# Fused band-and-summary attention with a GELU layer pair: the second layer of the last two chunks as seven products of quarters, and a new order of the early steps

## The chip, the core and the metric

The kernel runs on one core of a Trainium2 chip. The metric is the time of one launch in microseconds (us), measured on the device, as the median of several runs; lower is better. The core's engines work side by side from queues of their own: PE (TensorE, matmuls; its weight loads are listed apart as PEld), DVE (VectorE), ACT (ScalarE), POOL (GpSimd) and SP (SyncE, which here issues all transfers). Matmuls write to PSUM (tiles named `ps...`); the other tiles lie in SBUF.

## The reference

`q`, `k` and `v` have the shape 4 x 8 x 768 x 64 (batch, heads, positions, head width). Every query sees the keys less than 16 positions away and, besides, one summary of each block of 32 keys. The result, 3072 tokens of 512, goes through two layers with a GELU between.

```python
k_sum = k.reshape(B, H, nb, block, D).max(axis=3)
v_sum = v.reshape(B, H, nb, block, D).mean(axis=3)
scores_l = scale * np.matmul(q, k.transpose(0, 1, 3, 2))
scores_s = scale * np.einsum('bhsd,bhnd->bhsn', q, k_sum) + np.log(block)
scores_all = np.concatenate([np.where(mask_l, scores_l, -1e9), scores_s], axis=-1)
a = np.exp(scores_all - np.max(scores_all, axis=-1, keepdims=True))
a = a / (np.sum(a, axis=-1, keepdims=True) + 1e-09)
x = np.matmul(a, np.concatenate([v, v_sum], axis=2))       # to 3072 x 512
h = x @ w_in                                               # 512 x 2048
g = 0.5 * h * (1.0 + erf(h * inv_sqrt2))
out = g @ w_out                                            # 2048 x 512
```

## The kernel before

**Numbers.** Most operands of a matmul are f32 values split into two f16 values, a high part and the rest (`..._hi` on ACT, `..._lo` on DVE), and a product is three matmuls: high x high, high x low, low x high. The weights arrive as 64-bit floats and are put together on DVE in three steps of bit work each (`wi_bits`, `wo_bits`, lines 348 to 357).

**Tiles.** The attention is done in 24 units of 256 queries and 4 heads (`Unit`). The two units of 256 tokens make a chunk, so there are 12 chunks; six units make one of the four batches of the input. The attention of units 0 to 5 (`N_F32`) runs in f32 (`f_scores`, `f_sums`, `f_values`), that of the others in f16 pairs (`scores`, `sums`, `values`). Between them stand the maximum over partitions on POOL (`maximum`, L726), the shift on DVE (`shift`, L731), the exponent on ACT (`exponent`, L734) and the division (`norm_take`, `norm_rec`, `norm_spread` and `norm_mult` on DVE, L799 to L816). `x_hi` and `x_lo` (L820, L823) split the result.

**First layer.** Chunks 0 to 3 take `phase1` (L843 to L845): 24 matmuls of 256 columns for each of 8 blocks of `w_in`. Chunks 4 to 11 go in pairs (`STRASSEN`): the 512 tokens by 512 inputs of a pair are four quarters, and each part q of four (512 of the 2048 outputs) takes seven products `sp b q n` (L914, 12 matmuls of 256 columns each) in place of eight. Sums of inputs are `xsum`, `xs_hi`, `xs_lo`; sums of weights `wt_add`, `wt_hi`, `wt_lo`. The products of one part gather in three PSUM banks x, y and z; `snap` (ACT, L925) copies y in between, `comb` (DVE, L932) adds. Then `s_gelu` (L939), `sg_hi` (ACT, L942) and `sg_lo` (DVE, L946) put the result into `gg`.

**Second layer.** `phase2 c i` (L960 to L962) takes part i // 2 of chunk c for 128 of its 256 tokens: 12 matmuls of 512 columns. Eight such steps make a chunk; `store` (ACT, L967) copies the PSUM bank and `put` sends it.

**The order.** The string `ORDER` lists all steps by name. They are issued in that order, so it is the order of every engine's queue and of SP's transfers; waits between engines follow from the tiles. Buffers with a count (`f4k` has four) can be written again when the last reader of one is done.

**Front.** In the first 120 us the weights are made, the first units are computed and `phase1` begins. `fetch_w_in`, `fetch_k`, `fetch_v`, `fetch_vt` and `load_q`, `load_k`, `load_v` are transfers on SP's queue; `prep_k` and `prep_v` reduce blocks on DVE; `wi_diff` and `wi_dlo` make the low part of a weight block on PE and ACT in place of `wi_lo` on DVE.

## Time and profile before

| | us |
|---|---|
| median of three runs | 607.15 (604.36 to 607.5) |
| the profiled execution | 603.98 |
| its span, first to last instruction | 602.2 |
| PE busy, of the span | 578.3 (96%) |
| DVE busy | 420.2 (70%) |
| ACT busy | 351.1 (58%) |
| POOL busy | 90.2 (15%) |

The profile has one execution. Busy PE counts each matmul to its modelled end, and matmuls overlap: one of 512 columns is listed with 379 ns, while the next starts much sooner, so the time of a step on PE is read from start to start. The chain of waits follows back from the last instruction what released each one. `L960` is line 960 of the kernel. Groups are written as `line engine operation out<-in`, then the count, the busy time, the mean of one, and the idle time before them with what ended it.

### The profile page before, as it was taken

How to read it: one execution, taken by the hardware profiler on the slowest of the kernel's cores; microseconds unless marked ns; L12 is line 12 of the kernel's file. 1: busy time of each engine (PE TensorE's matmuls, PEld its weight loads, DVE VectorE, ACT ScalarE, POOL GpSimd, SP SyncE). 2: the span in 40 equal slices, each digit the busy share in tenths (PEclk: the TensorE clock that was granted, in tenths of full speed). 3: DMA queues.
4: the chain of work that ended last, by engine and by line, in shares of the span. 5: the costliest groups of instructions: out<-in, count | busy, mean ns of one | idle time of the engine just before them, and what ended most of it. 6: DMA issues, size and time to landing. Idle time of an engine off the chain costs nothing.

```text
span 602.2 us, 12775 instructions
## 1 busy us (share of the span) xinstructions
PE 578.3 (96%) x5532; PEld 378.2 (63%) x5532; DVE 420.2 (70%) x567; ACT 351.1 (58%) x508; POOL 90.2 (15%) x41
## 2 busy tenths in 40 slices
PE   3988989999999999999999999999999999999997
...
DVE  4999999798878889788978646956367655134110
...
GB/s 315 370 356 267 270 124 253 130 178 112 127 130 111 112 77 120 64 145 75 126 25 112 40 60 59 118 63 51 45 85 2 19 19 19 19 1 19 17 19 35
DMA packets 28216, 64.47 MB, mean 107 GB/s; under 512 B 2688, under 2 KB 6528, under 8 KB 28160
## 3 DMA queue, kind: packets, MB, share of 16 engines
...
q14 instruction: 13, 0.11, 0.1%
...
## 4 chain that ended last, share of the span: by engine, by line
PE 87%; DVE 6%; issue 3%; DMA 2%; POOL 1%; ACT 1%; SPq 0%; POOLq 0%; ACTq 0%; DVEq 0%
PE psy L914 14%; PE pso L960 14%; PE pso L962 14%; PE pso L961 14%; PE psz L914 7%; PE psh L843 4%; PE psh L844 4%; PE psh L845 4%; PE psx L914 4%; PE psv L779 3%; PE pss L703 2%; PE psv L792 2%; DMA v<-in_vw_dram 1%; DVE wt L353 1%; DMA x32s<-in_w_out_dram 1%
## 5 line engine op out<-in xcount | busy, mean ns | idle before, releaser
L960 PE MATMUL pso<-w_out_h,gg 128*128 128x512 f16 x384 | 145.7, 379 | 0.7 <-ACT ot L967 0.7
L962 PE MATMUL pso<-w_out_h,gg 128*128 128x512 f16 x384 | 145.5, 379 | 0.0
L961 PE MATMUL pso<-w_out_l,gg 128*128 128x512 f16 x384 | 145.5, 379 | 0.0
L726 POOL PARTITION_ALL_REDUCE m<-s x24 | 83.4, 3473 | 354.3 <-DVE s L717 126.0
L914 PEld LDWEIGHTS <-wt 128*128 128x128 f16 x768 | 74.4, 98 | 14.0 <-issue 1.7
L843 PE MATMUL psh<-xos,ww 128*128 128x256 f16 x256 | 70.3, 275 | 0.0
L844 PE MATMUL psh<-xos,ww 128*128 128x256 f16 x256 | 70.2, 274 | 0.0
L914 PE MATMUL psy<-xos,wt 128*128 128x256 f16 x576 | 69.9, 273 | 0.2 <-ACT ww L925 0.2
L845 PE MATMUL psh<-xos,ww 128*128 128x256 f16 x256 | 70.1, 274 | 0.0
L946 DVE SCALAR_TENSOR_TENSOR gg<-g,gg 128x512 f16<-128x512 f32 x64 | 45.6, 727 | 29.8 <-ACT gg L942 29.6
L962 PEld LDWEIGHTS <-gg 128*128 128x128 f16 x384 | 37.6, 98 | 45.3
L914 PEld LDWEIGHTS <-ww 128*128 128x128 f16 x576 | 55.2, 98 | 12.7 <-issue 2.5
L960 PEld LDWEIGHTS <-gg 128*128 128x128 f16 x384 | 37.5, 98 | 40.3 <-issue 0.8
L961 PEld LDWEIGHTS <-gg 128*128 128x128 f16 x384 | 37.6, 98 | 39.7 <-issue 1.0
L925 ACT ACTIVATE ww<-psy 128x512 f32<-128x512 f32 x48 | 28.0, 590 | 46.2 <-PE psy L914 44.6
L967 ACT ACTIVATE ot<-pso 128x512 f32<-128x512 f32 x24 | 14.3, 596 | 58.0 <-PE pso L962 58.0
L932 DVE TENSOR_TENSOR g<-psz,ww 128x512 f32<-128x512 f32 x32 | 22.0, 686 | 31.0 <-PE psz L914 26.1
L939 ACT ACTIVATE g<-g 128x512 f32<-128x512 f32 x48 | 29.8, 624 | 21.3 <-DVE g L932 21.1
L942 ACT ACTIVATE gg<-g 128x512 f16<-128x512 f32 x64 | 38.8, 622 | 3.5 <-PE pso L961 2.9
L731 DVE TENSOR_TENSOR s<-s,m 128x1024 f32<-128x1024 f32 x24 | 29.2, 1217 | 9.5 <-POOL m L726 9.5
L734 ACT ACT_TABLE_LOAD x20 | 25.7, 1283 | 10.6 <-DVE s L731 10.3
L799 DVE STREAM_TRANSPOSE dent<-psv 128x512 f32<-128x512 f32 x24 | 17.1, 712 | 17.0 <-PE psv L792 11.1
...
## 6 DMA issues: line engine op xcount, KB each, us to landing
...
gg<-in_w_in_dram SPq DMA_DIRECT2D x6, 1024.0 KB
...
vb<-in_vb_dram SPq DMA_DIRECT2D x12, 384.0 KB
xos<-in_w_out_dram SPq DMA_DIRECT2D x4, 1024.0 KB
```

What stands on the lines that cost most here:

```text
L726: nc.gpsimd.partition_all_reduce(out_ap=self.m32, in_ap=self.s32, channels=P, reduce_op=bass_isa.ReduceOp.max)
L731: nc.vector.tensor_tensor(out=self.s32, in0=self.s32, in1=self.m32, op=ALU.subtract)
L843: nc.tensor.matmul(ph[:, e, :], wh, xh, start=(k == 0), stop=False)
L844: nc.tensor.matmul(ph[:, e, :], wh, xl, start=False, stop=False)
L845: nc.tensor.matmul(ph[:, e, :], wl, xh, start=False, stop=(k == NCC - 1))
L914: nc.tensor.matmul(ps[:, e, :], ws, xx, start=(first and e == 0 and k == 0 and m == 0), stop=(k == 1 and m == 2), skip_group_check=True,)
L939: nc.scalar.activation(dst, src, AF.Gelu, scale=1.0 / (SC_X * SC_WI))
L942: nc.scalar.activation(g_part(o // 2, q, 0, slice(o % 2, 4, 2)), g32t[b, q, o], AF.Copy, scale=SC_G)
L946: nc.vector.scalar_tensor_tensor(out=g_part(o // 2, q, 1, fs), in0=g32t.pop((b, q, o)), scalar=SC_G, in1=g_part(o // 2, q, 0, fs), op0=ALU ...
L960: nc.tensor.matmul(p, gh, w_out_h[:, f, :], start=(f == 0), stop=False)
L961: nc.tensor.matmul(p, gh, w_out_l[:, f, :], start=False, stop=False)
L962: nc.tensor.matmul(p, gl, w_out_h[:, f, :], start=False, stop=(f == NFC - 1))
```

## The change

The second layer of chunks 10 and 11 (the last pair) is done by seven products of quarters too. For each part q the quarters of A are chunk 10 or 11 by even or odd blocks of 128 of the four in a part; those of B are the same blocks of `w_out` by left or right 256 columns. `so n q j` is product n for 128 tokens: 6 matmuls of 256 columns. All parts gather in four PSUM regions: x and w (the bank pair of the scores), y (that of `phase2`) and z (that of the attention's values). y is copied three times (`o_snap`), `o_sum` adds it to x, z and w, `o_out` is the last copy of y, and `o_put` sends a quarter's half.

The results of the GELU stay in f32 (`h32`) until their sums are made (`h_sum`), and then seven operands a part are split (`h_hi`, `h_lo`) instead of four. They go to rooms of `gg` that chunks 8 and 9 have left and to rooms of `wt`. The weight sums are added up from the high and low parts of `w_out` (`t_sum`, eight steps a part), split (`t_hi`, `t_lo`), and put into buffers that the attention has left: x32s, v32, vh and vl, q32, k32, qh and ql; `dent`, `ph` and `pl` hold them in between. `wo_diff` and `wo_dlo` are defined and not called.

Removed: 16 `phase2`, 4 `store`, 4 `put`, 12 `comb`, 16 each of `s_gelu`, `sg_hi` and `sg_lo`. Added: 56 `so`, 12 `h_comb`, 16 `h_gelu`, 16 `h_sum`, 28 `h_hi`, 28 `h_lo`, 32 `t_sum`, 16 `t_hi`, 16 `t_lo`, 3 `o_snap`, 4 `o_sum`, 2 `o_out`, 8 `o_put`. No other step is removed or added.

The order is new in two places. From the start to just behind `phase1 2 0` (`wo_bits 6 0`) the same steps stand in another order; from there to `xsum 3 1`, which opens the products of chunks 6 and 7, nothing is changed; and from there to the end the order is new.

```diff
-fetch_k 0 0, prep_k 0 0, k_pack 2, fetch_w_in 5 5, load_m16, f_mask 2, wi_bits 5 0, wi_bits 5 1, wi_bits 5 2, wi_hi 5,
-load_eye, load_q 2, f_scores 2, fetch_w_in 3 3, wi_bits 3 0, fetch_v 1 2, prep_k_end 0 0, wi_bits 3 1, prep_v 1 2,
-fetch_w_in 0 0, evac 2, maximum 2, load_q 0, wi_bits 3 2, fetch_k 0 1, wi_bits 0 0, f_mask 0, k_pack 0, wi_bits 0 1,
-wi_hi 3, shift 2, load_neg, wi_bits 0 2, fetch_v 1 0, f_scores 0, prep_v 1 0, fetch_w_in 7 3, evac 0, wi_hi 0, wi_diff
-3 1, wi_diff 0 1, maximum 0, wi_dlo 0 1, wi_diff 3 0, wi_dlo 3 0, prep_k 0 1, wi_bits 7 0, f_mask 1, load_q 1, wi_bits
-7 1, wi_diff 0 0, wi_bits 7 2, k_pack 1, f_scores 1, shift 0, exponent 0, fetch_w_in 2 2, load_ind, wi_bits 2 0,
-wi_bits 2 1, wi_hi 7, evac 1, maximum 1, f_sums 0, wi_dlo 0 0, fetch_vt 1, wi_bits 2 2, wi_hi 2, fetch_vt 0, wi_lo 7,
-sum_vt 0, sum_vt 1, norm_take 0, norm_rec 0, norm_spread 0, wi_lo 5, fetch_vt 2, fetch_w_in 4 4, shift 1, wi_bits 4 0,
-sum_vt 2, load_v 0, mean_vt, s_load_vs 0, k_pack 3, wi_diff 2 1, f_mask 3, f_values 0, wi_diff 2 0, prep_k_end 0 1,
-fetch_w_in 6 2, exponent 1, wi_bits 4 1, wi_bits 4 2, load_v 1, norm_mult 0, f_sums 1, s_load_vs 1, wi_bits 6 0,
-wi_bits 6 1, norm_take 1, norm_rec 1, wi_dlo 2 0, x_hi 0, x_lo 0, norm_spread 1, f_values 1, norm_mult 1, load_q 3,
-f_scores 3, fetch_w_in 1 1, wi_bits 1 0, wi_bits 1 1, load_v 2, exponent 2, x_hi 1, f_sums 2, fetch_k 1 3, norm_take
-2, prep_k 1 3, x_lo 1, evac 3, load_k 4, load_q 4, fetch_w_out 0 4, load_vs 2, f_mask 4, wi_dlo 3 1, f_values 2,
-wi_bits 6 2, maximum 3, fetch_k 1 1, wi_dlo 2 1, load_mask, k_pack 4, phase1 0 3, wi_hi 4, shift 3, norm_rec 2,
-exponent 3, phase1 0 5, wi_hi 6, wi_bits 1 2, wo_bits 0 0, wo_bits 0 1, gelu 0 3, fetch_w_out 1 5, gelu 0 5, f_scores
...
+fetch_k 0 0, prep_k 0 0, prep_k_end 0 0, fetch_w_in 5 5, load_m16, load_q 2, k_pack 2, f_mask 2, f_scores 2, wi_bits 5
+0, wi_bits 5 1, wi_bits 5 2, wt_add 5 0, wt_add 5 1, fetch_vt 0, wi_hi 5, load_eye, load_ind, fetch_w_in 0 0, wi_lo 5,
+k_sums 0 0, sum_vt 0, wt_add 5 2, evac 2, maximum 2, f_mask 0, load_neg, wi_bits 0 0, wi_bits 0 1, k_pack 0, wt_hi 5,
+wt_lo 5, load_q 0, f_scores 0, wi_bits 0 2, fetch_vt 1, fetch_k 0 1, prep_k 0 1, sum_vt 1, prep_k_end 0 1, shift 2,
+evac 0, maximum 0, wi_hi 0, shift 0, exponent 0, k_pack 1, exponent 2, wi_diff 0 0, fetch_vt 2, wi_diff 0 1,
+fetch_w_in 3 3, f_mask 1, load_q 1, fetch_w_in 2 2, sum_vt 2, mean_vt, load_v 0, f_sums 0, wi_bits 3 0, fetch_w_in 4
+4, wi_bits 3 1, f_scores 1, load_q 3, wi_bits 3 2, norm_take 0, wi_hi 3, s_load_vs 0, wi_diff 3 0, wi_bits 2 0,
+wi_bits 2 1, wi_bits 2 2, evac 1, wi_dlo 3 0, load_v 1, norm_rec 0, wi_hi 2, norm_spread 0, f_values 0, norm_mult 0,
+maximum 1, fetch_w_in 7 3, wi_diff 2 1, f_mask 3, wi_dlo 0 1, wi_diff 3 1, k_pack 3, x_hi 0, wi_bits 4 0, wi_bits 4 1,
+wi_dlo 0 0, x_lo 0, shift 1, exponent 1, s_load_vs 1, f_scores 3, wi_bits 4 2, f_sums 1, wi_hi 4, fetch_w_in 1 1,
+wi_bits 7 0, load_v 2, wi_bits 7 1, evac 3, f_values 1, wi_diff 2 0, wi_dlo 2 0, norm_take 1, maximum 3, norm_rec 1,
+norm_spread 1, norm_mult 1, x_hi 1, wi_bits 7 2, fetch_k 1 1, load_k 4, f_mask 4, fetch_w_out 0 4, x_lo 1, wi_dlo 2 1,
+f_sums 2, norm_take 2, prep_k 1 1, fetch_k 1 2, phase1 0 5, wi_hi 7, phase1 0 2, gelu 0 2, load_vs 2, f_values 2,
+shift 3, wi_lo 7, norm_rec 2, load_q 4, wi_lo 4, exponent 3, phase1 0 0, norm_spread 2, k_pack 4, wo_bits 0 0, wi_bits
+1 0, norm_mult 2, wo_bits 0 1, wi_bits 1 1, wo_bits 0 2, gelu 0 0, fetch_w_in 6 2, g_hi 0 0, gelu 0 5, f_scores 4,
...
+3, phase2 8 4, phase2 8 6, store 8 0, put 8 0, norm_rec 22, norm_spread 22, t_sum 0 3, snap 5 0 1, norm_mult 22, sg_hi
+4 3 2, sg_lo 4 3 2, sp 5 1 1, snap 5 1 1, xsum 5 1, xsum 5 3, phase2 9 1, phase2 9 3, xs_hi 5 1, t_sum 0 1, xs_hi 5 3,
+xs_lo 5 1, t_sum 0 0, xsum 5 2, xs_lo 5 3, phase2 9 5, xsum 5 4, phase2 9 7, xs_hi 5 4, h_comb 0 0, t_sum 0 2, t_sum 0
+4, t_hi 0 3, t_lo 0 3, xs_hi 5 2, xs_lo 5 2, t_sum 0 5, sp 5 0 6, t_hi 0 1, sp 5 0 5, t_hi 0 2, t_lo 0 2, snap 5 0 2,
...
+h_hi 3 22, h_sum 2 4, so 1 2 1, h_hi 2 4, h_lo 3 11, h_hi 2 2, h_lo 2 2, so 1 3 0, so 1 3 1, sp 5 3 3, h_lo 2 1,
+h_gelu 3 2, so 3 1 0, so 2 2 1, o_snap 1, so 6 0 0, so 3 1 1, t_sum 3 5, t_hi 3 2, t_lo 3 2, h_comb 3 1, h_gelu 3 1,
+so 6 0 1, so 6 1 0, so 6 1 1, so 6 2 0, h_lo 3 22, so 5 1 1, so 5 2 0, so 5 2 1, h_hi 3 12, h_lo 3 12, h_lo 2 4, so 3
+2 0, h_sum 3 1, h_sum 3 3, h_sum 3 2, h_hi 3 2, h_lo 3 2, t_hi 3 3, t_hi 3 1, so 6 2 1, t_lo 3 3, so 6 3 0, so 6 3 1,
+h_hi 3 3, o_snap 2, so 2 3 0, h_lo 3 3, so 2 3 1, so 7 0 0, h_sum 3 4, h_hi 3 4, h_lo 3 4, put 8 1, h_hi 3 1, t_lo 3
+1, h_lo 2 3, so 7 0 1, so 7 1 0, so 7 1 1, so 7 2 0, so 7 2 1, so 7 3 0, so 3 2 1, h_lo 3 1, so 3 3 0, so 7 3 1, so 5
+3 0, so 5 3 1, o_snap 3, so 4 0 0, t_sum 3 6, t_sum 3 7, t_hi 3 4, o_sum 0, o_put 0 1, so 4 1 0, so 4 2 0, o_sum 3,
+o_put 3 1, o_put 3 0, t_lo 3 4, o_sum 4, so 4 3 0, so 3 3 1, o_put 0 0, o_sum 1, o_put 1 0, o_put 1 1, o_out 0, so 4 0
+1, so 4 1 1, o_put 2 0, so 4 2 1, so 4 3 1, o_out 1, o_put 2 1
...
+    b12, t2w, t32f = {}, {}, {}
+    A_ROOM = {11: (0, 0), 12: (0, 1), 22: (1, 1), 1: (1, 0)}
+    def a_part(q, m, z):
+        if m in A_ROOM:
+            c, h = A_ROOM[m]
+            return gg[:, c, q, z, h : FQ : 2, :]
+        room = wt[:, 2 * q : 2 * q + 2].rearrange("p i n -> p (i n)").bitcast(F16)
+        i = (2, 3, 4).index(m) * 4 * CH + z * 2 * CH
+        return room[:, i : i + 2 * CH].rearrange("p (e j) -> p e j", e=2)
+    def h32(q, o):
+        if (L2, q, o) not in g32t:
+            t = wk.tile([P, WP], F32, tag="f4k", bufs=N_F4K, name=f"h32_{q}_{o}")
+            for n in range(2):
+                g32t[L2, q, o // 2 * 2 + n] = t[:, n * 512 : (n + 1) * 512].rearrange("p (e j) -> p e j", e=2)
+        return g32t[L2, q, o]
+    def h_comb(q, o):
+        n, y = {0: (1, "x"), 1: (2, "z"), 3: (3, "z")}[o]
+        nc.vector.tensor_tensor(
+            out=split8(h32(q, o)), in0=split8(acc[L2, q, y]), in1=snaps[L2, q, n], op=ALU.add
+        )
+    def h_gelu(q, o):
+        nc.scalar.activation(
+            h32(q, o), acc[L2, q, "y"] if o == 2 else h32(q, o), AF.Gelu, scale=1.0 / (SC_X * SC_WI)
+        )
+    def h_src(q, m):
+        return h32(q, {11: 0, 12: 1, 22: 3, 1: 3, 2: 0, 3: 2, 4: 1}[m])
+    def h_sum(q, n):
+        a11, a12, a21, a22 = (h32(q, o) for o in range(4))
+        out, in0, in1, op = (
+            (a22, a21, a22, ALU.add),
+            (a11, a22, a11, ALU.subtract),
+            (a21, a11, a21, ALU.subtract),
+            (a12, a12, a11, ALU.subtract),
+        )[n - 1]
+        nc.vector.tensor_tensor(out=flat2(out), in0=flat2(in0), in1=flat2(in1), op=op)
+    def h_hi(q, m):
+        nc.scalar.activation(a_part(q, m, 0), h_src(q, m), AF.Copy, scale=SC_G)
+    def h_lo(q, m):
+        nc.vector.scalar_tensor_tensor(
+            out=a_part(q, m, 1), in0=h_src(q, m), scalar=SC_G, in1=a_part(q, m, 0), op0=ALU.mult, op1=ALU.subtract
+        )
+    def b_part(q, h, n, z):
+        return (w_out_h, w_out_l)[z][:, q * FQ + h : (q + 1) * FQ : 2, n * CH : (n + 1) * CH]
+    def t_room(q, n, z):
+        if (n, q, z) not in t2w:
+            if n == 1:
+                x = flat2(x32s[:, (4, 0, 1, 2)[q]]).bitcast(F16)
+                t2w[n, q, 0], t2w[n, q, 1] = x[:, :512], x[:, 512:]
+            elif n == 2:
+                v = ld.tile([P, UH * CT, D], F32, tag="v32", bufs=N_V32, name=f"t2_{q}")
+                v = v.rearrange("p n d -> p (n d)").bitcast(F16)
+                for i in range(4):
+                    t2w[n, q // 2 * 2 + i // 2, i % 2] = v[:, i * 512 : (i + 1) * 512]
+            elif n == 3:
+                a = wk.tile([P, UCOLS], F16, tag="vh" if q % 2 else "vl", bufs=N_VH, name=f"t3_{q}")
+                t2w[n, q, 0], t2w[n, q, 1] = a[:, :512], a[:, 512:]
+            elif q > 1:
+                t2w[n, q, z] = wk.tile([P, QCOLS], F16, tag=("qh", "ql")[z], bufs=N_QH, name=f"t4_{q}_{z}")
+            else:
+                if q == 0:
+                    a = ld.tile([P, QCOLS], F32, tag="q32", bufs=N_Q32, name="t4_0")
+                else:
+                    a = ld.tile([P, KC * TQ], F32, tag="k32", bufs=N_K32, name="t4_1")
+                a = a.bitcast(F16)
+                t2w[n, q, 0], t2w[n, q, 1] = a[:, :512], a[:, 512:1024]
+        return t2w[n, q, z]
+    def t_sum(q, i):
+        def tmp(k):
+            tag = ("pl", "dent", "ph")[k]
+            if tag == "dent":
+                return wk.tile([P, NR * CH], F32, tag="dent", bufs=1, name=f"tw_{q}_{i}")
+            return wk.tile([P, UCOLS], F16, tag=tag, bufs=N_PH, name=f"tw_{q}_{i}").bitcast(F32)
+        def whole(k, h, n):
+            b12[q, k] = tmp(k)
+            nc.vector.tensor_tensor(
+                out=b12[q, k].rearrange("p (e j) -> p e j", e=2), in0=b_part(q, h, n, 0), in1=b_part(q, h, n, 1), op=ALU.add
+            )
+        def diff(k, i0, i1, op, n):
+            nc.vector.tensor_tensor(out=b12[q, k], in0=b12[q, i0], in1=b12[q, i1], op=op)
+            t32f[n, q] = b12[q, k]
+        if i == 0:
+            whole(0, 0, 1)
+        elif i == 1:
+            whole(1, 1, 1)
+        elif i == 2:
+            diff(1, 1, 0, ALU.subtract, 3)
+        elif i == 3:
+            whole(2, 0, 0)
+        elif i == 4:
+            diff(0, 0, 2, ALU.subtract, 1)
+        elif i == 5:
+            diff(2, 1, 2, ALU.add, 2)
+        elif i == 6:
+            whole(1, 1, 0)
+        else:
+            diff(1, 1, 2, ALU.subtract, 4)
+    def t_hi(q, n):
+        nc.scalar.activation(t_room(q, n, 0), t32f[n, q], AF.Copy)
+    def t_lo(q, n):
+        nc.vector.tensor_tensor(out=t_room(q, n, 1), in0=t32f[n, q], in1=t_room(q, n, 0), op=ALU.subtract)
+    def so(n, q, j):
+        m, w, y = {
+            1: (11, (0, 0), "y"),
+            2: (12, (1, 0), "x"),
+            3: (4, (1, 1), "w"),
+            4: (22, 4, "y"),
+            5: (1, 1, "z"),
+            6: (2, 2, "y"),
+            7: (3, 3, "y"),
+        }[n]
+        first = (L2, y) not in acc
+        if first:
+            if y == "y":
+                t = ps_o.tile([P, DM], F32, tag="pso", name="pso_y")
+            elif y == "z":
+                t = ps_v.tile([P, 2, NR * CH], F32, tag="psv", name="psv_z")[:, 0]
+            else:
+                if "s" not in acc:
+                    acc["s"] = ps_s.tile([P, UCOLS], F32, tag="pss", name="pss_x")
+                t = acc["s"][:, :512] if y == "x" else acc["s"][:, 512:]
+            acc[L2, y] = t.rearrange("p (e j) -> p e j", e=2)
+        ps = acc[L2, y]
+        js = slice(j * P, (j + 1) * P)
+        for e in range(2):
+            gh, gl = (a_part(q, m, z)[:, e, js] for z in range(2))
+            if isinstance(w, int):
+                wh, wl = (t_room(q, w, z).rearrange("p (e n) -> p e n", e=2)[:, e] for z in range(2))
+            else:
+                wh, wl = (b_part(q, *w, z)[:, e] for z in range(2))
+            for k, (g, ww_) in enumerate(((gh, wh), (gh, wl), (gl, wh))):
+                nc.tensor.matmul(
+                    ps[:, j, :], g, ww_, start=(first and e == 0 and k == 0), stop=(e == 1 and k == 2),
+                    skip_group_check=True,
+                )
+    OSC = 1.0 / (SC_G * SC_WO)
+    osn = {}
+    def o_snap(n):
+        osn[n] = g32_tile(("os", n))
+        nc.scalar.activation(flat2(osn[n]), flat2(acc[L2, "y"]), AF.Copy, scale=OSC)
+    def o_sum(o):
+        y, s = {0: ("x", 1), 4: ("z", 2), 3: ("z", 3), 1: ("w", 4)}[o]
+        osn["o", o] = osn[s]
+        if o == 4:
+            osn[4] = osn[2]
+        nc.vector.scalar_tensor_tensor(
+            out=flat2(osn[s]), in0=flat2(acc[L2, y]), scalar=OSC, in1=flat2(osn[s]), op0=ALU.mult, op1=ALU.add
+        )
+    def o_out(j):
+        if j == 0:
+            osn["o", 2] = g32_tile(("os", 5))
+        nc.scalar.activation(osn["o", 2][:, j], acc[L2, "y"][:, j], AF.Copy, scale=OSC)
+    def o_put(o, j):
+        r0 = (2 * L2 + o // 2) * CH + j * P
+        queue[0].dma_start(out=out[r0 : r0 + P, o % 2 * CH : (o % 2 + 1) * CH], in_=osn["o", o][:, j])
```

`xsum` and `xsrc` name the buffers `x32s` directly; they compute the same.

More of the change, by code (lines that the diff above doesn't have):

```diff
@@ L111 @@
+values 6, s_k_hi 8, k_lo 8, gelu 2 5, fetch_k 2 0, load_q 9, s_q_hi 9, phase2 0 6, store 0 0, norm_take 6, add_mask 7,
+norm_rec 6, norm_spread 6, q_lo 9, maximum 7, phase1 2 3, prep_k 2 0, shift 7, load_vs 7, v_hi 7, scores 8, load_k 9,
+v_lo 7, fetch_v 2 1, load_q 11, fetch_k 2 2, exponent 7, phase2 0 1, phase2 0 3, s_p_hi 7, norm_mult 6, put 0 0,
 add_mask 8, prep_k 2 2, s_k_hi 9, phase2 0 5, phase2 0 7, k_lo 9, g_hi 2 4, p_lo 7, values 7, g_lo 2 4, sums 7,
@@ new lines @@
+add_mask 17, values 16, prep_k_end 3 0, k_sums 3 0, sums 16, q_lo 18, xs_hi 3 3, maximum 17, xs_lo 3 3, sp 3 1 6, sp 3
+0 2, comb 3 0 0, phase2 4 1, phase2 4 3, norm_take 16, norm_rec 16, norm_spread 16, s_gelu 3 0 0, sg_hi 3 0 0, xsum 3
+4, load_k 19, shift 17, s_k_hi 19, k_lo 19, exponent 17, load_q 19, prep_v 3 1, xs_hi 3 4, xs_lo 3 4, load_v 18,
+s_q_hi 19, q_lo 19, sp 3 0 7, snap 3 1 2, phase2 4 5, put 5 0, phase2 4 7, sg_lo 3 0 0, scores 18, prep_v 3 3, load_vs
+18, sp 3 1 7, add_mask 18, store 4 1, put 4 1, phase2 5 1, snap 3 0 3, sp 3 0 4, v_hi 18, s_gelu 3 0 2, sg_hi 3 0 2,
```

174 lines of the change are left out of this document (87 added, 87 removed).

## The prediction

> **What bounds the kernel now.** I read the page's share by engine and by line of the chain that ended last, then its 40 slices, then the busy time by stretch over five cuts that I chose, then the chain itself piece by piece around its gaps.
>
> ```profile
> PE 87%; DVE 6%; issue 3%; DMA 2%; POOL 1%; ACT 1%; SPq 0%; POOLq 0%; ACTq 0%; DVEq 0%
> PE   3988989999999999999999999999999999999997
> DVE  4999999798878889788978646956367655134110
> ```
> ```profile
> 0.00:53.10 53.10, 39.36 (x287) 21.85 (x287) 44.62 (x49) 24.86 (x33) 17.79 (x18) 1.00 0.90 318
> 53.10:118.30 65.20, 61.03 (x631) 48.66 (x628) 59.95 (x82) 47.43 (x70) 15.41 (x7) 0.97 0.64 221
> 118.30:233.80 115.50, 115.50 (x1264) 74.57 (x1262) 102.32 (x138) 78.95 (x106) 19.64 (x6) 1.00 0.37 116
> 233.80:480.10 246.30, 244.65 (x2562) 163.52 (x2560) 176.61 (x246) 157.87 (x230) 37.36 (x11) 1.00 0.24 71
> 480.10:602.20 122.10, 117.76 (x801) 69.59 (x799) 36.66 (x56) 41.95 (x71) 0.00 (x0) 1.00 0.05 18
> ```
>
> The columns of the second fence are the stretch, its length, busy PE, weight loads, DVE, ACT and POOL, the granted clock, DMA share and GB/s. The cuts are the first product of the first layer (53.1), the last product ahead of the place where both orders have done the same steps (118.3), the first seven-product step (233.8) and the start of the tail (480.1). From 118.3 on PE is busy almost without a break: there a microsecond of PE work is a microsecond of time. Before 53.1 it is DVE: 44.62 us busy of the 48.1 since its first data came at 5.0 (first row, from the view of waits), and the chain runs down DVE:
>
> ```profile
> DVE ks_f L471 <- DMA w_out_l<-in_kp_dram: 5.0, 1, 5.0
> ```
> ```profile
> 49.24 0.61 DVE wt L348
> 49.88 1.23 DVE wt L353
> 51.10 0.62 DVE dent L799
> 51.73 0.85 DVE ks L471
> ```
>
> The DMA share of 0.90 makes transfers the second bound of that stretch. So the change has two places to act: PE work saved anywhere after 53.1, and DVE work taken out of the front.
>
> **The change: the seven products.** Sixteen `phase2` steps of chunks 10 and 11 go, 12 matmuls of 512 columns each, 192 in all. Fifty-six `so` steps of 6 matmuls of 256 columns come, 336 in all.
>
> ```profile
> 575.67 1.31 PE psx L914 x12
> ```
> ```profile
> 588.02 0.38 PE L960 MATMUL pso<-w_out_h,gg 128*128 128x512 f16 x1 [0.69 <-ACT ot L967]
> ...
> 592.55 0.38 PE L960 MATMUL pso<-w_out_h,gg 128*128 128x512 f16 x1
> ```
>
> The second fence holds the first and last of 22 starts in a row, so 4.53/21 = 0.2157 us for 512 columns. The first has twelve matmuls of 256 columns, each with its own 128x128 weights, in 1.31: 0.109 each. That is the form of `so`. 192 x 0.2157 = 41.4 goes, 336 x 0.109 = 36.7 comes: **-4.7 us**. The cover of the new matmuls is the weight load under them:
>
> ```profile
> L914 PEld LDWEIGHTS <-wt 128*128 128x128 f16 x768 | 74.4, 98 | 14.0 <-issue 1.7
> ```
>
> 98 ns beneath 109 leaves 11. Should a tenth of the load show (10 ns x 336), 3.4 of the 4.7 would be gone.
>
> What feeds the products stands on DVE and ACT of the tail. Rows of that stretch, by groups:
>
> ```profile
> L946 DVE SCALAR_TENSOR_TENSOR gg<-g,gg 128x512 f16<-128x512 f32 x21 | 14.0, 689 | 22.3 <-ACT gg L942 22.3
> L942 ACT ACTIVATE gg<-g 128x512 f16<-128x512 f32 x21 | 12.5, 621 | 0.2
> L875 DVE TENSOR_TENSOR x32s<-x32s 128x512 f32<-128x512 f32 x4 | 2.8, 690 | 0.1
> ```
>
> All new DVE steps work on 512 elements a partition. `h_sum` 16, `t_sum` 32, `t_lo` 16, twelve more `h_lo` than there were `sg_lo`, and 4 `o_sum`: 80 instructions x 0.69 = 55.2. `h_comb` replaces `comb` one for one. A `t_sum` that adds two f16 blocks into f32 is not in the trace. Below, it might take half of a row, 0.35, which would save 16 x 0.35 = 5.6 of DVE; above, the 0.85 that `prep_k` took in the chain, for 768 elements, would add 32 x 0.16 = 5.1. I take 0.69, the like f32 row; neither end reaches PE, as follows. DVE has 36.7 busy in 122.1; it gets 91.9 in 122.1 - 4.7 = 117.4 and keeps **25.5 us free**. ACT gets 12 `h_hi` and 16 `t_hi` at 0.62, and five reads of PSUM for four `store`: 42.0 + 17.4 = about 59, half its time. I count both at nothing, covered by PE; what they cost without the cover is a rival below.
>
> The new waits on PE are the three `o_snap`: the next product into the same bank waits for ACT to copy it. Behind that matmul all of PE is queued. Between the last write and the next stand one `sp` and two `so` for the first (2.6 us) and two `so` for the others (1.3). The copy at the very end shows the price: 0.30 from the start of the last matmul to the copy, and 0.60 for it (second row below), 0.9 together. Covered; without the cover 3 x 0.9 = 2.7. The rooms bring waits too. `h_hi` writes into `gg` where chunks 8 and 9 are read and waits for their `phase2` of the same part; behind it on ACT stand `snap` and `h_gelu`, for which the next `sp` wait. `t_sum` of a part writes where `t_hi` and `t_lo` of the part before read; behind it on DVE stand `h_lo`, for which `so` waits. In the written order each has several PE steps between, so I count them at nothing; their price is the rival of the tail. `store 8 1`, which must empty that bank first, has seven steps of 6.5 us between. On SP eight `o_put` of half a block replace four `put`; nothing is queued behind them but one another. The end keeps its shape:
>
> ```profile
> 598.33 0.23 PE pso L962
> 598.63 0.60 ACT ot L967
> ```
>
> After the last matmul come 3.6 us of copy and store. The last copy is half as wide (0.3 us less) and the last `so 4` of part 3 stands near its late weights (`t_lo 3 4` after `o_sum 3`, about 0.3). I set these to 0.
>
> **The early order.** Which DVE steps stand ahead of `x_lo 1`, the last input of the first first-layer product? Out of the front go `prep_v 1 2`, `prep_v 1 0`, two thirds of the bit work of w_in blocks 6 and 1, `wi_lo 7`, `norm_take 2` and `prep_k 1 3`; into it come `wt_add 5` and `wt_lo 5`.
>
> ```profile
> L520 DVE TENSOR_REDUCE vs<-vb 96x32 f32<-96x1024 f32 x12 | 14.4, 1199 | 0.0
> L348 DVE TENSOR_SCALAR wst<-x32s 128x1024 int32<-128x1024 int32 x4 | 2.7, 685 | 0.0
> L425 DVE SCALAR_TENSOR_TENSOR wt<-t,wt 128x1024 f16<-128x1024 f32 x8 | 9.7, 1214 | 2.9 <-ACT wt L422 2.9
> L417 DVE TENSOR_TENSOR t<-wt,t 128x256 f32<-128x256 f32 x16 | 6.7, 416 | 0.2
> ```
>
> Out: 2 x 1.2 + 2 x (0.69 + 1.23) + 1.2 for `wi_lo 7` (as `wt_lo`, the same form) + 0.6 and 0.85 for the last two, by the chain above, = 8.9. In: 0.69 + 2 x 0.42 + 1.21 = 2.7. Net 6.2 us less. Against it stands a wait. `shift 0` now follows `shift 2` at once, and `maximum 0` cannot begin before `evac 0`.
>
> ```profile
> 15.12 5.46 POOL L726 PARTITION_ALL_REDUCE m<-s  x1 [13.15 <-ACT s L713]
> 23.05 3.70 POOL L726 PARTITION_ALL_REDUCE m<-s  x1 [2.47 <-DVE wt L357]
> ```
>
> In before, DVE fills the second of these (23.05 to 26.75) with other work; now `shift 2` ends near 23 and everything behind `shift 0` on DVE waits to about 26: 3 us, at most the whole 3.7. Before, DVE had 53.1 - 5.0 - 44.6 = 3.5 idle, nearly all of it behind its first transfers; with 1.4 of that left, as the weight sums of block 5 bridge a part (my estimate), the new front has 4.4. So of the 6.2 I count 5.3: the first `phase1` at 47.8. By then `f_values 2` has not been done, which before stood ahead of it, 1.1 us of PE (the row of 69.73 below); so PE has lost 4.2 less. SP's queue allows it.
>
> ```profile
> gg<-in_w_in_dram SPq DMA_DIRECT2D x6, 1024.0 KB
> vb<-in_vb_dram SPq DMA_DIRECT2D x12, 384.0 KB
> ```
>
> Up to `load_v 1` before sends 13.6 MB, after 11.0, by the sizes of the page's part 6 (two `vb` of 384 KB and two w_in of 1024 KB move behind, a q of 256 KB ahead): at 318 GB/s 43 against 34.5 us.
>
> How much survives to 118.3? All steps ahead of it are the same, so DVE's sum is too; only its idle time differs. It has those 3.5 idle before 53.1 and 65.2 - 60.0 = 5.2 to 118.3; the new order can remove about the second, as PE feeds it earlier. `x_lo 5` then ends some 5 us earlier, and `phase1 2 0` started 1.1 after it. After that both orders are equal, DVE 102.3 busy of 115.5: room, but little. One wait of the middle may go as well:
>
> ```profile
> 87.24 0.71 DVE L799 STREAM_TRANSPOSE dent<-psv 128x512 f32<-128x512 f32 x1
> ```
> ```profile
> 69.73 1.15 PE psv L622 x32
> ...
> 85.38 2.68 issue
> 88.05 1.86 PE psv L622 x32
> 89.91 0.33 PE psh L843
> 90.24 0.21 PE psh L844
> ...
> 91.86 0.11 PE psh L843
> ```
>
> The values of unit 4 wait here 2.68 us: they start 0.1 after the transpose of the same PSUM tile, `norm_take 4`, which stood on DVE behind bit work. The new order puts only `k_lo 6` close ahead of it, so a wait of about 1 (0.3 to the copy, as above, and 0.71) would be left. Bounds of the early order: 0 if the all-reduces cost what the DVE steps gave; 4.2 + 2.7 + 1.6 (below) = 8.5 if this gap goes too. I take **-4.5**, near the 4.2 worked out. The gap has a price behind it: after the gap matmuls ran 0.21 apart, not 0.11, until 91.86, which cost about 1.6 us. [...]
>
> **The rest of the order.** From the fourth attention batch on, steps are reshuffled too. Of 233.8 to 480.1 PE shows 246.30 - 244.65 = 1.65 idle, and restarts after waits add a little. At best 3 goes, at worst a like sum comes; I take **-1.0**.
>
> Sum: -4.7 - 4.5 - 1.0 = -10.2. The profiled execution took 603.98 us, 1.8 over its span of 602.2: 593.8 after. The three timed runs had a median of 607.15 (604.36 to 607.5); from that, 596.9. The forecast stands between, nearer the median: **596.0**.
>
> **Rivals.** Forecast, 55%.
> *The front gives nothing* (0, not 4.5): the two all-reduces in a row and the transfers eat it; the wait on `shift 0` speaks for it, the 6.2 us of DVE work against. 600.5; 15%.
> *The gap goes too* (8.5): 592.0; 10%. For it the place of `norm_take 4`; against it the thin room of DVE to 233.8.
> *The tail turns to DVE, mildly.* The 28 `h_lo` and 16 `t_lo` each follow an ACT step. In the tail of before a `sg_lo` waited 22.3/21 = 1.06 us on average. DVE has 25.5 free: it becomes the bound from 25.5/44 = 0.58 a pair. At 0.75 it needs 33, 7.5 over: 603.5; 9%.
> *The tail turns to DVE, in full*: at 1.06 the waits are 46.7, 21 over: 617; slower from 0.90 a pair on. For it: in-order queues, and each late pair delays the next. Against it: those waits were of an engine 70% idle, and the new order puts `t_sum` steps between. 5%.
> *The products don't save*: the weight loads show (3.4 above): 599.4; 6%.
>
> Faster by over 0.5% (what a measurement can tell from no change) means under 604.1: the forecast but for its edge, the first two, the last, and half of the mild tail, 0.83; within, 0.11; slower, 0.06. The range leaves out the full tail at the top and the best combination of all terms at the bottom: 588 to 604.
>
> **What would show it.** Right: the first `psh` matmul of `phase1` near 48 us; PE whole from about 113; no idle on PE over 1 us in the tail; `so` twelve in 1.31; DVE some 92 us busy in the last 117. Wrong: DVE busy without gap in the tail and PE waiting for it, a granted clock under 1 there, or first `phase1` after 52.

## The result, and the profile after

The changed kernel takes 591.22 us (median of four runs, 590.31 to 591.98); the kernel before 606.84 (four runs, 604.36 to 607.5). The ratio is 0.9759, with an interval of 0.9729 to 0.9789: faster by 15.6 us. The forecast was 596.0 (588 to 604): right in direction and range, 4.8 us too high. In the profiled executions the time went from 603.98 to 591.23, and the span from 602.2 to 589.4, 12.8 less.

The page's chain by engine and its slices for PE and DVE, of the changed kernel:

```profile
PE 86%; DVE 9%; DMA 2%; ACT 1%; issue 1%; POOL 1%; SPq 0%; POOLq 0%; DVEq 0%; ACTq 0%
PE   4989989999999999999999999999999999999997
DVE  5799998999978889788879747873668567499863
```

Busy time by stretch, cut at the same places of the work as before: the first product of the first layer (45.7), `phase1 2 0` (111.0), the first seven-product step (226.8), the start of the tail (here taken at 469).

```profile
0.00:45.70 45.70, 34.57 (x255) 18.53 (x256) 35.80 (x44) 25.50 (x36) 14.90 (x17) 1.00 0.88 317
45.70:111.00 65.30, 62.42 (x660) 49.31 (x659) 61.77 (x82) 45.58 (x65) 16.16 (x8) 0.97 0.71 238
111.00:226.76 115.76, 115.70 (x1262) 74.57 (x1262) 104.58 (x143) 82.02 (x110) 19.65 (x6) 1.00 0.41 127
226.76:469.00 242.24, 241.39 (x2582) 161.33 (x2580) 176.59 (x249) 155.13 (x230) 37.20 (x11) 1.00 0.25 73
469.00:589.40 120.40, 116.06 (x925) 86.05 (x923) 83.92 (x132) 52.39 (x94) 0.00 (x0) 1.00 0.05 19
```

The last ten slices of DVE, 7655134110 before, now read 8567499863, and PE beside them stays whole. The first product starts at 45.7 instead of 53.1, `phase1 2 0` at 111.0 instead of 118.3; from there to the first seven-product step both kernels need the same (115.8 and 115.5 us). So the front gives 7.0 to 7.4 us by these starts. To see the rest, I took PE's idle time: the start of a step, less the matmul time of all steps ahead of it, each at the shortest that this kind of step takes in either trace.

| | before | after | difference | forecast |
|---|---|---|---|---|
| matmul time of all steps | 561.7 | 557.0 | -4.7 | -4.7 |
| PE idle ahead of the first seven-product step | 30.5 | 23.5 | -7.0 | -4.5 |
| from there to `phase2 8 4` | 4.9 | 4.1 | -0.8 | -1.0 |
| in the tail | 1.2 | 1.5 | +0.3 | 0 |
| behind the last step | 3.8 | 3.3 | -0.5 | 0 |

Sum -12.7, of 12.8 in the spans. The first row counts every matmul at its shortest time, so what a slower one costs would show as idle time in the rows below it; the tail has 0.3 more. The medians differ by 2.9 us more than the spans. The executions of the kernel before vary more: over all its runs the mean granted clock lay between 0.988 and 0.997 and the time between 602.7 and 609.0, and the profiled one, with 0.997, was among the shorter. Those of the changed kernel lay at 0.997 to 1.0, and between 590.0 and 592.0.

The seven-product steps in the tail, from the chain of waits (start, length, what), the groups of the two sums of weights, and all that PE waited for in the tail, from the view of waits (in total, times, longest):

```profile
580.35 2.62 PE pso_y L1148 x24
...
583.62 2.63 PE pso_y L1148 x24
```
```profile
L1092 DVE TENSOR_TENSOR tw<-tw,tw 128x512 f32<-128x512 f32 x16 | 11.0, 689 | 0.3
...
L1087 DVE TENSOR_TENSOR tw<-w_out_h,w_out_l 128x512 f32<-128x512 f16 x16 | 10.9, 684 | 0.1
```
```profile
PE psy L937 <- ACT ww L948: 1.2, 1, 1.2
```

2.62/24 = 0.109 us for a matmul: the weight loads beside them, 98 ns each, do not show. One wait over 0.3 us is left in the tail, at `sp 5 1 1`, and none is at a `so`.

### The profile page after: what moved, and what is told of

It reads as the page before. It is cut to its first block, busy times and chain, and to the rows that moved or that the text cites. A ratio compares the mean times of both kernels' runs of the same rounds, so it can differ in the third digit from the quotient of the medians.

```text
span 589.4 us, 13159 instructions
## 1 busy us (share of the span) xinstructions
PE 570.1 (97%) x5676; PEld 389.8 (66%) x5676; DVE 462.7 (78%) x647; ACT 360.6 (61%) x533; POOL 87.9 (15%) x41
## 4 chain that ended last, share of the span: by engine, by line
PE 86%; DVE 9%; DMA 2%; ACT 1%; issue 1%; POOL 1%; SPq 0%; POOLq 0%; DVEq 0%; ACTq 0%
PE psy L937 15%; PE pso L983 12%; PE pso L984 12%; PE pso L985 12%; PE psz L937 7%; PE psx L937 4%; PE pso_y L1148 4%; PE psh L866 4%; PE psh L867 3%; PE psh L868 3%; PE psv L802 3%; PE pss L726 2%; PE pss_x L1148 2%; PE psv L815 2%; DMA w_out_l<-in_mask_dram 1%; DMA w_out_l<-in_kp_dram 1%
## 5 line engine op out<-in xcount | busy, mean ns | idle before, releaser
L749 POOL PARTITION_ALL_REDUCE m<-s x24 | 82.1, 3422 | 341.0 <-DVE s L740 149.8
L983 PE MATMUL pso<-w_out_h,gg 128*128 128x512 f16 x320 | 121.4, 379 | 0.0
L984 PE MATMUL pso<-w_out_l,gg 128*128 128x512 f16 x320 | 121.3, 379 | 0.0
L985 PE MATMUL pso<-w_out_h,gg 128*128 128x512 f16 x320 | 121.3, 379 | 0.0
L937 PEld LDWEIGHTS <-ww 128*128 128x128 f16 x576 | 55.4, 98 | 14.8 <-issue 2.9
L985 PEld LDWEIGHTS <-gg 128*128 128x128 f16 x320 | 31.3, 98 | 37.7
L948 ACT ACTIVATE ww<-psy 128x512 f32<-128x512 f32 x48 | 28.0, 590 | 45.7 <-PE psy L937 43.7
L983 PEld LDWEIGHTS <-gg 128*128 128x128 f16 x320 | 31.3, 98 | 33.0 <-issue 0.4
L984 PEld LDWEIGHTS <-gg 128*128 128x128 f16 x320 | 31.3, 98 | 31.9
L969 DVE SCALAR_TENSOR_TENSOR gg<-g,gg 128x512 f16<-128x512 f32 x48 | 34.4, 730 | 11.7 <-ACT gg L965 11.5
L955 DVE TENSOR_TENSOR g<-psz,ww 128x512 f32<-128x512 f32 x24 | 16.5, 688 | 29.1 <-PE psz L937 22.9
L962 ACT ACTIVATE g<-g 128x512 f32<-128x512 f32 x36 | 22.2, 624 | 18.2 <-DVE g L955 18.1
L757 ACT ACTIVATE s<-s 128x1024 f32<-128x1024 f32 x24 | 25.3, 1055 | 9.1 <-DVE s L754 8.8
L866 PEld LDWEIGHTS <-ww 128*128 128x128 f16 x256 | 25.4, 99 | 7.2 <-issue 2.8
L965 ACT ACTIVATE gg<-g 128x512 f16<-128x512 f32 x48 | 29.4, 623 | 1.2 <-PE pso L984 0.4
L867 PEld LDWEIGHTS <-ww 128*128 128x128 f16 x256 | 25.3, 99 | 4.6 <-issue 0.5
```

Of the source, the lines that this page charges most:

```text
L749: nc.gpsimd.partition_all_reduce(out_ap=self.m32, in_ap=self.s32, channels=P, reduce_op=bass_isa.ReduceOp.max)
L866: nc.tensor.matmul(ph[:, e, :], wh, xh, start=(k == 0), stop=False)
L867: nc.tensor.matmul(ph[:, e, :], wh, xl, start=False, stop=False)
L937: nc.tensor.matmul(ps[:, e, :], ws, xx, start=(first and e == 0 and k == 0 and m == 0), stop=(k == 1 and m == 2), skip_group_check=True,)
L965: nc.scalar.activation(g_part(o // 2, q, 0, slice(o % 2, 4, 2)), g32t[b, q, o], AF.Copy, scale=SC_G)
L969: nc.vector.scalar_tensor_tensor(out=g_part(o // 2, q, 1, fs), in0=g32t.pop((b, q, o)), scalar=SC_G, in1=g_part(o // 2, q, 0, fs), op0=ALU ...
```

## The experiments

**One part of the change at a time.** The first takes the changed kernel and puts the first 329 steps of its order back as they were; the second takes the kernel before and gives it only the new 329.

```diff
-fetch_k 0 0, prep_k 0 0, prep_k_end 0 0, fetch_w_in 5 5, load_m16, load_q 2, k_pack 2, f_mask 2, f_scores 2, wi_bits 5
+fetch_k 0 0, prep_k 0 0, k_pack 2, fetch_w_in 5 5, load_m16, f_mask 2, wi_bits 5 0, wi_bits 5 1, wi_bits 5 2, wi_hi 5,
...
```

> The changed kernel with the early order of before (all steps up to the place where both orders have done the same); the rest is the changed one's. Theory: the microseconds that PE lost in the front come back and stay to the end, since PE has no idle time behind it in which they could be caught up: first product of the first layer near 53 us, PE idle ahead of phase1 2 0 about 30 in place of 22.7, span 589.4 + 7.0 = 596.4, time about 598. Rival: DVE, 102 to 105 busy of 116 us behind the front, sets the pace there, so a later front is caught up or an earlier one was given back: span under 592.

> The kernel before with the early order of the changed one and nothing else. Theory: the front is worth the same without the seven products: span 602.2 - 7.0 = 595.2, time about 597. Rival (the front is worth something only with the new middle and tail): span over 599.

Measured: 600.53 us (597.32 to 601.78), ratio 0.992 (0.9888 to 0.9952), span 596.7; and 596.99 (596.76 to 598.44), ratio 0.9867 (0.9844 to 0.989), span 595.0. The new front alone is worth 1.33% (8.1 us), all the rest alone 0.8% (4.6 to 4.9 us); 0.992 x 0.9867 = 0.9788, at the edge of the 0.9729 to 0.9789 of both together. PE's idle time up to `phase1 2 0` was 30.1 us with the old front and 22.5 with the new, whatever the tail. So the two parts stand apart, and about half of the gain is the front.

**The middle.** From `xsum 3 1` to `phase2 8 4` the order of before, then the tail of the changed kernel.

```diff
-xsum 3 1, x_lo 13, sp 3 1 2
+xsum 3 1, xsum 3 3, s_q_hi 18
...
```

> The changed kernel with the order of before from xsum 3 1 to the last step ahead of phase2 8 4; the steps that this leaves follow in the changed kernel's order. Theory: the new middle is worth the 0.8 us of PE idle time that lie between the two traces there (4.9 against 4.1): span 589.9 to 590.7. Rival: the new middle also makes the attention of the last units early enough for the weight sums, and without it the tail starts late: span over 592.

Measured: 600.48 (599.81 to 601.05), ratio 0.9936 (0.992 to 0.9951): 9.3 us over the changed kernel. The same stretch of both, in the columns of the windows, the changed kernel first:

```profile
470.00:480.00 10.00, 10.00 (x111) 6.56 (x109) 6.23 (x9) 3.65 (x7) 0.00 (x0) 1.00 0.01 2
```
```profile
470.00:480.00 10.00, 5.71 (x72) 2.84 (x70) 6.70 (x12) 8.30 (x12) 0.00 (x0) 0.94 0.00 0
```
```profile
481.48 2.50 PE L937 MATMUL psx<-xos,ww 128*128 128x256 f16 x11 [3.54 <-DVE xos L846]
```

In the old order the exponent of unit 22 runs at 473.6, in the new one at 450.7. The new tail wants that unit's values, and ahead of them, for `sp 5 0 2`, the low part of unit 21: `x_lo 21` comes at 481.4 instead of 466.1, and PE stands at the seam (last row). The middle saves 0.8 us of its own, but the tail needs it.

**Matmul time taken out.** The third of the three matmuls for each pair of blocks is left out of `so`: 112 fewer, 12.2 us.

```diff
-            for k, (g, ww_) in enumerate(((gh, wh), (gh, wl), (gl, wh))):
+            for k, (g, ww_) in enumerate(((gh, wh), (gh, wl))):
...
```

> The changed kernel in which the products so leave out the third of their three matmuls (low part of the GELU times high part of the weights): 112 matmuls of 256 columns fewer; everything that DVE and ACT make stays. Theory: PE is the bound of the tail, so 112 x 0.109 = 12.2 us go: span 577.2. Rival: the operands on DVE and ACT are as late as PE is, and less than half is gained: span over 583.5.

Measured: 585.82 (585.21 to 586.65), ratio 0.9678 (0.9657 to 0.97); span 583.4, so 6.0 of the 12.2. The longest wait of PE in its tail, and the chain ahead of it:

```profile
PE pso_y L1148 <- ACT wt L1042: 3.4, 1, 3.4
```
```profile
563.69 0.60 DVE wt L1045
564.29 0.61 DVE h L1039
...
564.93 0.70 DVE h L1039
...
565.65 0.70 DVE h L1039
...
566.38 0.64 ACT wt L1042
...
567.06 1.36 PE pso_y L1148 x8
```

Behind an `h_lo` (first row) these are the three `h_sum` of part 3, `h_hi 3 2` and `so 6 3 0`. In the changed kernel itself the last input of that step was ready 1.1 us before its start (0.4 at the closest, `so 4 3 0`). At its closest steps the tail is balanced to a microsecond: half of this saving was lost, 3.4 us of it in a wait that leads back to DVE.

**DVE work added in the tail.** Each `t_lo` twice, and in another kernel each `h_lo` too; the result is the same.

```diff
+        for _ in range(2):
+            nc.vector.tensor_tensor(out=t_room(q, n, 1), in0=t32f[n, q], in1=t_room(q, n, 0), op=ALU.subtract)
```

> The changed kernel with each h_lo and each t_lo done twice (the same result): 44 more DVE instructions of 0.69, 30.4 us, in the tail, where DVE is 83.9 us busy of 120.4. Theory: the free time of DVE there can be used, so 114.3 fit and at most 2 us come: span 589.4 to 591.5. Rival: much of the free time is waiting for ACT and PE in a fixed order and cannot be used, so DVE becomes the bound: 8 us or more, span over 597.

> The changed kernel with each of the 16 `t_lo` done twice: 16 x 0.69 = 11.0 us more on DVE in the tail, same result. By the forecast, which left DVE 25.5 us free there, nothing is added (0 to 0.5 us). By the theory that some 9 us of that are usable wherever they lie (30.4 us added cost 21.2), 2 us are added. By the theory that work ahead of a waiting product costs in proportion from the first microsecond (0.70 a microsecond), 7.7 us are added.

Measured: with 30.4 us more on DVE 614.54 (612.4 to 618.78), ratio 1.0161 (1.0109 to 1.0212), span 610.6, 21.2 over; with 11.0 us more 596.47 in a single run, span 594.7, 5.3 over. (The fronts of these two executions ended 0.4 us earlier and 0.5 later than the changed kernel's, by the start of `phase1 2 0`, so the tail's own part is nearer 21.6 and 4.8.) PE's waits in the tail, with 30.4 and with 11.0:

```profile
PE psy L937 <- ACT ww L948: 10.2, 3, 7.0
PE pso_y L1150 <- DVE wt L1046: 2.0, 2, 1.1
PE pso_y L1150 <- ACT wt L1042: 1.5, 1, 1.5
```
```profile
PE psy L937 <- ACT ww L948: 4.7, 3, 2.0
PE pso_y L1149 <- DVE wt L1045: 0.4, 1, 0.4
```

What PE waits for longest is on ACT, but the cause is DVE. ACT and DVE of the first kernel around the wait of 7.0:

```profile
557.15 0.69 DVE L1039 TENSOR_TENSOR h<-h 128x512 f32<-128x512 f32 x1
```
```profile
557.87 0.63 ACT L1042 ACTIVATE gg<-h 128x512 f16<-128x512 f32 x1 [1.36 <-DVE h L1039]
558.41 0.58 ACT L948 ACTIVATE ww<-psy 128x512 f32<-128x512 f32 x1
```
```profile
559.04 2.72 PE L937 MATMUL psy<-xos,wt 128*128 128x256 f16 x12 [7.02 <-ACT ww L948]
```

`h_hi 2 1` waits on ACT for `h_sum 2 1` on DVE; behind it in ACT's queue stands `snap 5 3 2`, which needs nothing of DVE and which `sp 5 3 7` waits for. This is the wait through a queue that the forecast had named. Neither theory had the size of the smaller kernel right (2 or 7.7 expected, 5.3 came): the first 11.0 cost 0.48 a microsecond, the next 19.4 cost 0.82. The two lots stand at different places, so these rates are not one curve. But there is no stock of free time that is used up first: already the first 11.0 us cost time, with DVE idle for a third of the tail.

**What stretches DVE in the front.** First come 3.1 us of extra DVE work ahead of `x_lo 1`: the bit work of block 2 twice.

```diff
-wi_bits 2 0, wi_bits 2 1, wi_bits 2 2
+wi_bits 2 0, wi_bits 2 1, wi_bits 2 2, wi_bits 2 0, wi_bits 2 1, wi_bits 2 2
```

> The changed kernel with the three bit steps of w_in block 2 done twice (the same result): 3.1 us more of DVE work ahead of x_lo 1. Theory: DVE's work in the front is time, one for one: first phase1 at 48.8 (45.7 before), span 592.0 to 592.5. Rival: DVE's idle time up to 111 us (4.7 before the first phase1, 3.5 behind it) takes it up: span under 590.5.

Measured: 600.52 (597.29 to 601.87), ratio 0.993 (0.9904 to 0.9957): 9.3 us over the changed kernel, three times what was added, and 10.7 in the spans. The expectation was wrong on that, and DVE's rows say why (POOL's first, then DVE's):

```profile
33.09 3.77 POOL L750 PARTITION_ALL_REDUCE m<-s  x1 [8.15 <-DVE wt L371]
47.65 3.22 POOL L750 PARTITION_ALL_REDUCE m<-s  x1 [10.79 <-ACT s L737]
```
```profile
30.57 1.23 DVE L367 SCALAR_TENSOR_TENSOR wt<-gg,wt 128x1024 int32<-128x1024 int32 x1
...
33.81 2.80 DVE L367 SCALAR_TENSOR_TENSOR wt<-gg,wt 128x1024 int32<-128x1024 int32 x1
...
47.79 1.78 DVE L828 TENSOR_SCALAR rc<-dent 128x16 f32<-128x16 f32 x1
```

The same instruction, 1.23 us at 30.57, takes 2.80 at 33.81, beside an all-reduce; one of 0.17 us takes 1.78 beside the next. The longer work had pushed them there. Over all DVE steps up to `phase1 2 0` the durations add up to 119.3 us, against 110.2 in the changed kernel: 3.1 put in, 6.0 stretched; DVE reached the end of these steps 10.6 later. The rest is idle time, 1.4 more, in which PE has a part: DVE waited 0.65 for its `psv` at 47.04, and the granted clock was 0.80 between 33 and 53 us here, 1.00 in the changed kernel's profile. So this run, planned as a price of DVE work, found the second cause of the front's gain.

To see it by itself, `wi_bits 0 2` is moved into an idle time of DVE beside the first all-reduce.

```diff
-load_neg, wi_bits 0 0, wi_bits 0 1, k_pack 0, wt_hi 5, wt_lo 5, load_q 0, f_scores 0, wi_bits 0 2, fetch_vt 1,
+load_neg, wi_bits 0 0, wi_bits 0 1, wi_bits 0 2, k_pack 0, wt_hi 5, wt_lo 5, load_q 0, f_scores 0, fetch_vt 1,
```

> The changed kernel with `wi_bits 0 2` (1.21 us) moved ahead of `wt_lo 5`, into the 1.51 us in which DVE waits beside the first all-reduce on POOL; nothing else differs. If a DVE instruction of this kind and an all-reduce that run side by side hold each other up, the moved step takes about 2.8 us instead of 1.21 (or `wt_lo 5`, just behind it, does), and the all-reduce 5.1 to 5.5 us instead of 3.59. If the long instructions of the kernel before come from the transfers (DMA share 0.9) or from which buffers are read, both keep their 1.2 and 3.6 us. The time of the end stays within 1 us in both cases, as DVE then waits for `fetch_k 0 1` until 21.2 anyhow.

Measured: 591.12 in one run; the time is as expected. The moved step and the all-reduce in this kernel, then the same step in the changed one, then the step that held this place in the kernel before:

```profile
15.74 2.80 DVE L370 SCALAR_TENSOR_TENSOR wt<-gg,wt 128x1024 int32<-128x1024 int32 x1
```
```profile
15.21 3.58 POOL L749 PARTITION_ALL_REDUCE m<-s  x1 [13.23 <-ACT s L736]
```
```profile
18.52 1.21 DVE L370 SCALAR_TENSOR_TENSOR wt<-gg,wt 128x1024 int32<-128x1024 int32 x1
```
```profile
17.54 2.80 DVE L353 SCALAR_TENSOR_TENSOR wt<-gg,wt 128x1024 int32<-128x1024 int32 x1
```

The instruction is held up, 2.80 for 1.21, and it does not lengthen the all-reduce (3.58, as the 3.59 of the changed kernel, where 5.1 to 5.5 was expected). So place alone stretches a DVE step here. That the all-reduce of before took 5.46 has another cause; the last section has what the times of the traces say of it.

**The two waits that are left.** `f_values 4` ahead of `norm_take 4`; `sp 5 1 1` behind `phase2 9 1`; both; and the changed kernel once more on the chip of the last.

```diff
-f_sums 4, norm_take 4, g_hi 1 5, prep_k_end 1 0, norm_rec 4, g_hi 0 4, f_values 4,
+f_sums 4, g_hi 1 5, prep_k_end 1 0, g_hi 0 4, f_values 4, norm_take 4, norm_rec 4,
...
-sg_lo 4 3 2, sp 5 1 1, snap 5 1 1, xsum 5 1, xsum 5 3, phase2 9 1,
+sg_lo 4 3 2, xsum 5 1, xsum 5 3, phase2 9 1, sp 5 1 1, snap 5 1 1,
```

> The changed kernel with f_values 4 issued ahead of norm_take 4 and norm_rec 4 (they follow it). In the changed kernel PE waits 2.2 us there for norm_take 4, and runs 1.7 us longer behind at the slow clock. Theory: in this stretch DVE is the bound, since phase1 2 0 (111.03) starts with the end of x_lo 5 (111.56), so the 3.9 us only move to phase1 2 0: less than 0.5 us gained, span 588.9 or more. Rival: DVE's own idle time there (3.1 us ahead of shift 5, for POOL) shrinks with it, and most of the wait is gained: span 585.5 to 587.5.

> The changed kernel with sp 5 1 1 and snap 5 1 1 behind phase2 9 1, whose 2.59 us of PE work then stand in the wait of 1.34 us ahead of sp 5 1 1. Theory: the wait is for a PSUM bank alone and goes: span 588.1. Rival: the steps behind it (operands of the tail) are as late, and the wait comes back at another step: span 589.2 or more.

> The changed kernel with two small moves: the matmuls of `f_values 4` ahead of `norm_take 4`, and the product `sp 5 1 1` behind `phase2 9 1`. If the gap of 2.2 us at `f_values 4` with its 1.7 us of slow matmuls behind it, and the wait of 1.3 us at `sp 5 1 1`, are time of the end and nothing else takes their place, this is the fastest of all kernels here: 591.2 less 2.7 (what the first move gave in the median) less 1.0 (the second) = about 587.5. If DVE's sum up to `phase1 2 0` is the bound there, the first move only shifts the wait, as the profile of that kernel hinted (0.9 us at `phase1 2 0`), and the time stays within 1 us of the changed kernel's.

> The changed kernel once more, as a measure for the run with both moves on the same chip. 591.2 if nothing differs between chips; both theories on the two moves are read against this time.

Measured: 588.53 (587.15 to 591.85), ratio 0.9752 (0.9727 to 0.9777); 590.17 (589.78 to 593.76), ratio 0.9779 (0.9755 to 0.9802); both 588.69 (587.32 to 589.83), ratio 0.9718 (0.9696 to 0.974); the changed kernel again 591.11 (590.01 to 591.8), ratio 0.9759 (0.9738 to 0.9779). Each move alone cannot be told from the changed kernel by its ratio; with both, every run lies below every run of the changed kernel on the same chip: 2.4 us, and the lowest ratio of all kernels here that leave no work out. The traces show 1.3 of it (spans 589.3 and 588.0): the wait at `f_values 4` is gone, but `phase1 2 0` waits 1.4, and `phase2 9 1` waits 0.85 in the place of the 1.34 at `sp 5 1 1`. What `phase1 2 0` waits for is not `x_lo 5`, as the first expectation has it: that ends only 0.5 us behind its start (111.56 and 111.03 in the changed kernel). The chain of the changed kernel shows the way:

```profile
109.16 0.61 DVE x32s L839
...
109.79 0.63 ACT xos L843
110.42 0.57 ACT g L875
...
111.03 0.27 PE psh L866
```

These are `norm_mult 5` on DVE, `x_hi 5` and behind it in ACT's queue `gelu 1 3`, which empties a PSUM tile of the first layer, and `phase1 2 0`. With both moves this chain came only 0.8 earlier. So DVE holds the end of the front, through ACT's queue. The profiled executions of the two single moves (spans 590.1 and 592.0) tell less: in both the granted clock was 0.91 between 33 and 53 us, and the first product came at 49.6 and 48.7.

Why the slow matmuls behind `f_values 4` cost nothing can be read from the changed kernel's two profiled executions. The wait was there in both; the first one, then the second, in the stretch that follows the first product:

```profile
75.36 2.17 issue
77.53 1.15 PE psv L645 x32
78.68 0.21 PE psh L866
```
```profile
45.70:111.00 65.30, 61.55 (x663) 48.56 (x660) 61.66 (x83) 46.24 (x68) 18.33 (x8) 1.00 0.76 248
```

In the first the granted clock fell behind the wait (0.97 over the stretch, matmuls 0.21 apart instead of 0.11); in the second, with PE idle for 2.2 us between 70 and 100 (2.2 in the first as well), it stayed at 1.00. `phase1 2 0` started at 111.0 in the one and at 110.9 in the other: the second waited 1.5 there for the same chain from DVE.

## Why the prediction was right, and where not

**The products: right.** -4.7 forecast, -4.7 measured; 0.109 a matmul; a `t_sum` that adds two f16 blocks takes 0.684, the value taken. The rival in which weight loads show is out.

**The early order: the term was mis-sized, and one step of its working was wrong.** -4.5 forecast, -7.0 in the profiles, 8.1 in the medians when done alone. The failed step is "All steps ahead of it are the same, so DVE's sum is too; only its idle time differs". It was the other way round: DVE's idle time up to `phase1 2 0`, behind its first data, was 8.7 before and 8.2 after, and the durations of the same steps fell from 114.6 to 110.2. Before, four steps ahead of `x_lo 1` (it included) took 3.9 us more than after: two of bit work 2.80 and 1.61 (1.23 and 0.69 after), `norm_rec 0` 1.37 (0.42), `x_lo 1` 1.12 (0.68). With the old order put back into the changed kernel the four are long again (2.80, 1.61, 1.37, 0.92), and the moved step (2.80 for 1.21) shows that place beside an all-reduce is enough. `norm_mult 5`, from which the chain to `phase1 2 0` starts, ended 5.7 us earlier (109.8, before 115.5), and PE, which before came 2.8 behind it without a wait, now comes 1.3 behind it. The second error was the 3 us priced on `shift 0`: it cost nothing.

```profile
15.26 3.59 POOL L749 PARTITION_ALL_REDUCE m<-s  x1 [13.28 <-ACT s L736]
21.57 3.22 POOL L749 PARTITION_ALL_REDUCE m<-s  x1 [2.72 <-ACT s L736]
```
```profile
23.66 1.22 DVE L754 TENSOR_TENSOR s<-s,m 128x1024 f32<-128x1024 f32 x1
```

The second all-reduce was over at 24.8, and `shift 2` on DVE (last row), held by an earlier transfer, at 24.9; `shift 0` followed without a wait. That DVE's idle time ahead of the first product still came near the 4.4 taken (4.7, by the windows) is luck: it lies elsewhere, 1.5 ahead of `wt_lo 5` and 1.45 for a transfer. Its busy time there fell by 8.8 (44.6 to 35.8), where 6.2 was counted, and so the first product came at 45.7, not 47.8. The rival "front gives nothing" is out.

**"The gap goes too": no.** About 1 us was to be left at `f_values 4`; 2.2 stayed. Its price was wrong too: taken as 2.7 + 1.6, its removal brought `phase1 2 0` forward by 0.8 us in the traces (2.4 in the medians, with both moves), since the chain from DVE is late next.

**The rest of the order: right in size, wrong in meaning.** -0.8 where -1.0 was taken; without it the tail loses 9 us, a dependence that the forecast did not see.

**The tail: right that nothing waits, wrong on the reserve.** DVE was to be 91.9 busy of 117.4; it was 83.9 of 120.4 (last row of the windows). Mostly this is because an instruction that follows another at once ends 0.60 to 0.61 behind it (first two rows of that chain without the third matmuls) and not 0.69: the lengths of all in this stretch add up to 90.1. But "keeps 25.5 us free" was used as if all of it could be filled, and the rival's threshold of 0.58 a pair came from it. Doubling the pairs adds 0.69 for each; by that rule it costs 30.4 - 25.5 = 4.9, or nothing with the 36.5 that were free. It cost 21.2; the 11.0 cost 5.3. The mechanism of that rival was right; its threshold was far too high.

**The sum.** -10.2 by terms, -12.8 measured, and the forecast then went up to 596.0 towards the median of before. From the profiled 603.98 the terms gave 593.8, nearer to 591.2.
